# Dilated q and k of the first batch loaded as fp32 by two other queues, and a new order of the work, in a fused sliding-window attention and gated feed-forward kernel

## The chip, the cores and the metric

The kernel runs on one core of a Trainium2 chip. The metric is the device time of one execution in microseconds (us); before the change it is 302.36 us, the median of three runs (302.0 to 302.91). The core has a matrix engine (TensorE, PE in the profile), a vector engine (VectorE, DVE), a scalar engine (ScalarE, ACT), GpSimd (POOL) and a sync engine (SyncE, SP). DMAs are issued by POOL, SP or ACT.

## The reference

Eight batches of eight heads, 576 positions, 64 values per head. Heads 0 to 3 look back over a plain window of 32 positions, heads 4 to 7 over a dilated one: 128 positions back, each fourth of them. The result, 4608 tokens of 512 values, goes through a feed-forward layer with a gate.

```python
def _attn_ref(q, k, v):
    scores = scale * np.matmul(q, k.transpose(0, 1, 3, 2))
    mask_plain = (rel >= 0) & (rel < window)                 # window = 32
    mask_dil = (rel >= 0) & (rel < window * dilation) & (rel % dilation == 0)   # dilation = 4
    ...
    attn = attn / (np.sum(attn, axis=-1, keepdims=True) + 1e-09)
    return np.matmul(attn, v).astype(np.float32)

def _moe_ref(x, w_in, w_out, beta):
    h = x @ w_in                                             # 512 -> 2048
    g = h * (1.0 / (1.0 + np.exp(-beta * h)))
    return (g @ w_out).astype(np.float32)                    # 2048 -> 512
```

## The kernel before

**The feed-forward part** goes over nine tiles of 512 tokens. For each tile, `slot_h` (L904) makes 16 groups: four matmuls (L913; for the first four groups of the first tile six, of parts of the tokens, so 72 instructions in that tile) add up one bank of h from xT (the attention's result, transposed) and w_in; ACT makes a tanh of it (L922), DVE the gate g (L927). A bank of PSUM is held from the first matmul to the end of the gate. `block` (L936) then makes the output of 128 tokens: 16 matmuls (L948, "o") from g and w_out, the first eight with the first half of w_out, the others with the second; an eviction to osb on ACT or DVE (L963, L965) and a store by SP (L968).

**The attention part** runs batch by batch and is laid into the feed-forward matmuls, since a tile of tokens needs its batch's result. For batches 0 to 2 q and k are loaded by row (`direct_qk`, L428, into the tiles st: a dilated part std, a plain part stp), by POOL with a cast from fp32 to bf16 in the DMA. PE transposes them in groups of 36 small matmuls (dilated L500, plain L510); ACT and DVE copy the halves to kT, qT, dk, dq (L262, which is the helper `copy`). Then come scores on PE (dilated L709, plain L773, tail L678), exps on ACT (L645), masks on DVE or POOL (L649; for the first batch PE adds them to the scores, L699, L759, L762), values on PE (dilated L814, plain L830, tail L799), a normalization on DVE (L664, L665), and for batches 0 and 1 transposes back on PE (L852, L867, L882) with copies to xT. From batch 2 on the way back goes by DMA. From batch 3 on, q and k are cast into DRAM by POOL's DMAs and transposed by SP's. The plain values (vp, `direct_vp`, L444) lie in rows of 96 positions with a halo of 32, which DVE or POOL copies on chip once they have landed.

**What sets the order.** Nothing is issued by hand. Each piece is a `plan.op` with its possible engines, guessed durations, dependencies and a due time (`vt`); `Plan.run` (L78) goes through them with a guessed clock of each engine, picks the next piece by time and due time, and so writes the order of each engine's instructions. CAPS (L46) limits how many PSUM banks a kind of work holds at once (of eight in all). NUDGE (L48) shifts the guessed start of single pieces by their number. Where PE would have nothing to do in the first 80 us of that guess, `filler` (L1060) puts in a matmul of zeros (L1061). The order is fixed when the program is built; on the chip each engine goes through its list and waits for what each instruction needs. At most eight DMAs of POOL's queue are open at a time: the ninth waits for the first one's landing.

**The loads of the start.** POOL's DMAs come in this order: dilated q, plain k, plain q, the dilated values (vd), two halves of the plain ones (vp); then batch 1's dilated k, w_in in three pieces (512, 512 and 1024 columns), the two halves of w_out, the tail values (vt), then batch 1's dilated q, plain k and plain q, its values, and so on. Only the dilated k rows of the first batch go another way: `first_keys` (L434) loads them as fp32, half by SP and half by ACT, into a part of the second g buffer (free at that time), and ACT and DVE cast each half to bf16. SP issues beta ahead of its half.

## Time and profile before

| | |
|---|---|
| median of three runs | 302.36 us |
| the profiled execution | 302.0 us, of which the span is 300.3 us |
| mean granted clock of TensorE | 0.994 |
| busy: PE, DVE, ACT, POOL | 291.0, 183.8, 168.8, 86.4 us |
| first h matmul; first o matmul | 20.10; 34.13 us |
| queue 0 (POOL's): bytes moved | 18.58 MB |
| fillers (L1061) | 45 |

The span runs from the first instruction to the last. A line of the table of groups names the source line, the engine, the operation, output and input tiles, the count, then busy time and mean duration, then the idle time of the engine just before these instructions and what ended it. A busy share can hide waits, since matmuls overlap; the start of one set of matmuls and that of the next tell more. In the tables by stage the share of DMA is a sum over transfers that overlap and can exceed 1.

### The profile page before, as it was taken

What the parts mean: (1) busy time and instruction counts of PE and PEld (TensorE: products, weight loads), DVE (VectorE), ACT (ScalarE), POOL (GpSimd) and SP (SyncE); (2) the same over time, 40 slices, a digit from 0 to 9 for tenths busy, and PEclk for the clock granted to TensorE, in tenths of its full rate; (3) what the DMA queues carried; (4) which work ended last, traced back from release to release, by engine and by line L of the source; (5) the groups of instructions that cost most, each with busy time, mean ns of one, the idle gap of its engine ahead of it and who ended that gap; (6) DMA issues with size and microseconds to landing.
All of it is one profiled execution on the core that took longest, in us unless ns stands there. A gap on an engine that the chain in (4) does not pass through costs nothing.

```text
span 300.3 us, 6262 instructions
## 1 busy us (share of the span) xinstructions
PE 291.0 (97%) x2430; PEld 148.2 (49%) x2466; DVE 183.8 (61%) x425; ACT 168.8 (56%) x310; POOL 86.4 (29%) x125
## 2 busy tenths in 40 slices
PE   6999999999999999999999999999999999999995
PEld 3665455645454444544545454445454444444454
DVE  4686667788767756786669365946485047543300
ACT  2677667876567643854386347733674158554311
POOL 8776356384337012710182046200000000000000
PEclk9799999999999999999999999999999999999999
DMA  7999999579999999999999989996203400000122
GB/s 153 183 208 207 202 178 214 144 104 157 200 193 184 149 176 149 199 184 167 180 178 135 224 185 192 145 191 155 76 20 97 110 35 35 2 36 35 56 86 70
DMA packets 111009, 42.00 MB, mean 140 GB/s; under 512 B 87636, under 2 KB 103652, under 8 KB 110980
## 3 DMA queue, kind: packets, MB, share of 16 engines
q0 software_dynamic: 60016, 18.58, 60.0%
q1 hardware_dynamic: 50676, 22.66, 36.3%
q8 instruction: 19, 0.31, 0.4%
q10 hardware_dynamic: 288, 0.36, 0.4%
q14 instruction: 10, 0.08, 0.1%
HBM read 37.76 MB, written 18.87 MB: 189 GB/s over the span
## 4 chain that ended last, share of the span: by engine, by line
PE 94%; DMA 2%; DVE 2%; issue 1%; ACT 0%; DVEq 0%; POOLq 0%
PE bank L948 41%; PE bank L913 41%; DMA st<-in_q_dram 2%; PE bank L830 2%; PE bank L709 2%; PE bank L814 1%; PE bank L1061 1%; PE bank L737 1%; PE bank L500 1%; PE bank L510 1%; PE bank L773 1%; PE bank L799 1%; PE bank L678 1%; DVE xdm L665 1%; DVE pt L649 0%
## 5 line engine op out<-in xcount | busy, mean ns | idle before, releaser
L948 PE MATMUL bank<-w_out_bf,g 128*128 128x512 bf16 (+2 forms) x585 | 132.2, 367 | 1.9 <-issue 1.1
L913 PE MATMUL bank<-xT,w_in_bf 128*128 128x512 bf16 (+2 forms) x571 | 132.2, 376 | 0.6
L927 DVE SCALAR_TENSOR_TENSOR g<-tnh,bank 128x512 bf16<-128x512 bf16 x144 | 95.4, 683 | 53.8 <-ACT tnh L922 52.6
L922 ACT ACTIVATE tnh<-bank,beta_half 128x512 bf16<-128x512 f32 x144 | 96.4, 688 | 50.7 <-PE bank L913 40.6
L913 PEld LDWEIGHTS <-w_in_bf 128*128 128x128 bf16 x584 | 55.7, 98 | 62.5 <-issue 0.3
L948 PEld LDWEIGHTS <-g 128*128 128x128 bf16 x608 | 55.2, 98 | 57.9 <-issue 0.2
L963 ACT ACTIVATE osb<-bank 128x512 f32<-128x512 f32 (+1 forms) x31 | 18.2, 592 | 42.9 <-PE bank L948 40.9
L645 ACT ACTIVATE pt<-bank 128x384 bf16<-128x384 f32 (+1 forms) x54 | 21.0, 464 | 3.8 <-PE bank L737 2.2
L645 ACT ACTIVATE ptd<-bank 128x512 bf16<-128x512 f32 x32 | 17.0, 600 | 8.9 <-PE bank L709 8.8
L649 DVE TENSOR_TENSOR pt<-pt,mask_n 128x384 bf16<-128x384 bf16 (+1 forms) x40 | 13.9, 364 | 12.7 <-ACT pt L645 12.3
L665 DVE TENSOR_TENSOR xsp<-bank,rcp 96x384 bf16<-96x384 f32 x32 | 17.7, 554 | 1.1
L421 POOL DMA_DIRECT2D vt<-in_v_dram x16 | 16.7, 1116 | 0.9 <-PE bank L799 0.9
L664 DVE RECIPROCAL rcp<-bank 128x4 f32<-128x4 f32 (+2 forms) x72 | 12.8, 178 | 5.5 <-PE bank L814 3.4
L649 DVE TENSOR_TENSOR ptd<-ptd,mask_d 128x512 bf16<-128x512 bf16 x28 | 11.2, 421 | 7.7 <-ACT ptd L645 7.1
L665 DVE TENSOR_TENSOR xdm<-bank,rcp 128x256 bf16<-128x256 f32 x32 | 13.6, 424 | 1.1
L965 DVE TENSOR_SCALAR osb<-bank 128x512 f32<-128x512 f32 (+2 forms) x7 | 4.2, 595 | 16.1 <-PE bank L948 16.1
L421 POOL DMA_DIRECT2D vp<-in_v_dram x9 | 11.2, 1249 | 7.2 <-DVE g L927 4.2
L421 POOL DMA_DIRECT2D s<-in_q_dram x10 | 12.6, 1264 | 0.3 <-issue 0.3
L1027 POOL COPY pace<-xT 1x2 bf16<-1x2 bf16 x4 | 0.7, 176 | 41.3 <-DMA xT<-x 41.3
L421 POOL DMA_DIRECT2D s<-in_k_dram x10 | 12.2, 1220 | 0.9 <-issue 0.9
L1061 PE MATMUL bank<-zero 128*128 128x256 bf16 x45 | 9.7, 331 | 1.1 <-DVE warm L321 1.1
L830 PEld LDWEIGHTS <-pt 128*128 128x128 bf16 x192 | 8.6, 97 | 4.4 <-DVE pt L649 0.3
(115 smaller groups left out, 176.2 us busy)
## 6 DMA issues: line engine op xcount, KB each, us to landing
out_dram<-osb SPq DMA_DIRECT2D x35, 256.0 KB, 6.3
s<-in_k_dram POOLq DMA_DIRECT2D x10, 288.0 KB, 10.0
s<-in_q_dram POOLq DMA_DIRECT2D x10, 288.0 KB, 8.5
w_out_bf<-in_moe_w_out_dram POOLq DMA_DIRECT2D x2, 1024.0 KB, 18.5
vp<-in_v_dram POOLq DMA_DIRECT2D x7, 288.0 KB, 13.4
st<-in_q_dram POOLq DMA_DIRECT2D x6, 288.0 KB, 6.8
x<-xsp SPq DMA_DIRECT2D x12, 144.0 KB, 5.2
st<-in_k_dram POOLq DMA_DIRECT2D x5, 288.0 KB, 7.2
```

What stands on the lines that cost most here:

```text
L421: {"POOL": nc.gpsimd, "SP": nc.sync, "ACT": nc.scalar}[queue].dma_start(out=out, in_=in_)
L645: nc.scalar.activation(out=w(), in_=sc(), func=ACT.Exp, scale=SCALE)
L649: E[e].tensor_tensor(out=w(), in0=w(), in1=m(), op=ALU.mult)
L664: nc.vector.reciprocal(out=r, in_=p[..., D])
L665: nc.vector.tensor_tensor(out=dst, in0=p[..., 0:D], in1=r.unsqueeze(len(p.shape) - 1).to_broadcast(list(p.shape[:-1]) + [D]), op=ALU.mult)
L830: nc.tensor.matmul(pv[:, a, h2, :], lhsT=lhs, rhs=vp[kv][:, (2 * x + h2) * NI + 3 * j + a, 0:D + 1], start=True, stop=True)
L913: nc.tensor.matmul(bank(g)[:, a:z], lhsT=w_in_bf[:, kt, fb * P:(fb + 1) * P], rhs=xT[:, kt, xo + a:xo + z], start=(i == 0 and kt == kts[0] ...
L922: nc.scalar.activation(out=th[:, 0:n], in_=bank(g)[:, 0:n], func=ACT.Tanh, scale=beta_half[:, fb:fb + 1])
L927: nc.vector.scalar_tensor_tensor(out=g_t[t % 2][:, fb, c0:c0 + n], in0=th[:, 0:n], scalar=1.0, in1=bank(g)[:, 0:n], op0=ALU.add, op1=ALU.mult)
L948: nc.tensor.matmul(bank(g)[:, lo:hi], lhsT=g_t[t % 2][:, fb, tb * P:(tb + 1) * P], rhs=w_out_bf[:, fb, lo:hi], start=(fb == 0), stop=(fb = ...
L963: nc.scalar.mul(out=ob[:, lo:hi], in_=bank(g)[:, lo:hi], mul=0.5)
L1061: nc.tensor.matmul(BANKS[b][:, 0:256], lhsT=zero[:, 0:P], rhs=zero[:], start=True, stop=True)
```

## The change

1. The dilated q rows of the first batch are loaded like the k rows: as fp32, half by SP and half by ACT, into the next five blocks of the second g buffer, then cast on chip. `first_keys` becomes `first_rows(z)`; q's due time is put just behind k's.
2. The due time of the two w_out loads goes from -7.27 to -7.2, so behind the loads of batch 1's q and k rows (-7.25).
3. h may hold three PSUM banks at once, no longer four.
4. NUDGE is another list of shifts (about a hundred of them, for other pieces).

```diff
-    CAPS = {"h": 4, "p": 4, "o": 3, "z": 4, "a": 8, "s": 5, "w": 6}
+    CAPS = {"h": 3, "p": 4, "o": 3, "z": 4, "a": 8, "s": 5, "w": 6}
-    NUDGE = {7: -400, 18: -2500, 19: -900, 33: -60, 47: -2500, 49: 400, 54: 400, 55: -150, 62: 60,
+    NUDGE = {6: -150, 10: -2500, 17: -900, 19: 400, 22: -150, 27: -2500, 40: -900, 52: 2500, 54: -900,
...
-    def first_keys():
+    def first_rows(z):
-        stage = g_t[1][:, 0:5, :].rearrange("p f n -> p (f n)").bitcast(FP32)[:, 0:RD * D]
-        src = bass.AP(tensor=k.tensor, offset=k[0, 4].offset, ap=[[RD * D, P], [1, RD * D]])
+        stage = g_t[1][:, 5 * z:5 * z + 5, :].rearrange("p f n -> p (f n)").bitcast(FP32)[:, 0:RD * D]
+        src = bass.AP(tensor=(k, q)[z].tensor, offset=(k, q)[z][0, 4].offset, ap=[[RD * D, P], [1, RD * D]])
...
-                        lambda e, x=x: copy(e, std[0][:, part[x]], stage[:, part[x]]),
-                        [load(("SP", "ACT")[x], (stage[:, part[x]], src[:, part[x]]), [], -9.1, 288, .41, 400, 1200)],
-                        -9.1, sbuf=True) for x in range(2)]
+                        lambda e, x=x: copy(e, std[z][:, part[x]], stage[:, part[x]]),
+                        [load(("SP", "ACT")[x], (stage[:, part[x]], src[:, part[x]]), [], -9.1 + .02 * z, 288, .41, 400, 1200)],
+                        -9.1 + .02 * z, sbuf=True) for x in range(2)]
...
-        ld[0]["qk", z, h0] = first_keys() if n == 0 else direct_qk(0, z, h0, [], -9 + .01 * n)
+        ld[0]["qk", z, h0] = first_rows(z) if h0 else direct_qk(0, z, h0, [], -9 + .01 * n)
...
-                 [], -7.27 + .01 * n, 2048, .41)
+                 [], -7.2 + .01 * n, 2048, .41)
```

In the program that is built, this moves on each engine:

- POOL issues plain k, plain q, the values, w_in in three pieces, then batch 1's dilated k, the tail values, batch 1's dilated q, plain k and plain q, then the first half of w_out; the second half follows behind the masks and batch 1's dilated values, and batch 1's plain values follow that. Three memsets for the second batch's values stand early, ahead of the identity matrix.
- SP issues k, q and then beta; ACT issues k and q ahead of its table load. DVE casts three of the four halves, ACT one.
- PE transposes dilated k, plain k, dilated q, plain q, and then makes all 16 dilated scores of the first batch. Batch 1's transposes and scores stand between the h groups 8 to 13 of the first tile, where the old order has them between the first o matmuls; the first o follows after 60 h instructions instead of 68. There are 52 fillers instead of 45: 35 ahead of the first h (37 before) and 17 behind it (8 before), of which eight stand ahead of h group 8, five and two in batch 1's scores.
- From batch 3 on the order of kinds is alike; o matmuls and h groups are more finely mixed.

## The prediction

> **What bounds the kernel now.** I began with the page: busy times, then the slices.

> ```profile
> PE 291.0 (97%) x2430; PEld 148.2 (49%) x2466; DVE 183.8 (61%) x425; ACT 168.8 (56%) x310; POOL 86.4 (29%) x125
> ...
> PE   6999999999999999999999999999999999999995
> ...
> PEclk9799999999999999999999999999999999999999
> DMA  7999999579999999999999989996203400000122
> ```

> TensorE (PE) is busy everywhere but in the first and last slice; the DMA engines are full up to about 50 us and slack later. The costliest groups say what PE does:

> ```profile
> L948 PE MATMUL bank<-w_out_bf,g 128*128 128x512 bf16 (+2 forms) x585 | 132.2, 367 | 1.9 <-issue 1.1
> L913 PE MATMUL bank<-xT,w_in_bf 128*128 128x512 bf16 (+2 forms) x571 | 132.2, 376 | 0.6
> ...
> L1061 PE MATMUL bank<-zero 128*128 128x256 bf16 x45 | 9.7, 331 | 1.1 <-DVE warm L321 1.1
> ```

> h (L913) and o (L948) hardly ever wait. In the chain of waits, four of either take 0.86 us late in the run, 0.216 each, and no line of another engine is there for long after 73 us. So nothing can be won after some 60 us; what can change lies in front. The table by stage:

> ```profile
> 0.00:20.00 20.00, 16.59 (x329) 11.00 (x330) 13.02 (x48) 11.18 (x25) 16.09 (x37) 0.91 1.17 178
> 20.00:40.00 20.00, 19.84 (x151) 10.41 (x153) 12.71 (x24) 12.40 (x21) 10.15 (x15) 1.00 1.24 205
> 40.00:60.00 20.00, 19.41 (x424) 11.82 (x417) 15.62 (x45) 16.02 (x40) 9.92 (x15) 1.00 1.27 176
> ```

> (PE, weight loads, DVE, ACT, POOL, then clock, DMA share, GB/s.) The timeline of PE gives the marks that I count from:

> ```profile
> 7.78 0.48 PE L500 MATMUL bank<-turn,st 64*64 64x64 bf16 x36 [1.92 <-DMA st<-in_q_dram]
> ...
> 20.10 0.38 PE L913 MATMUL bank<-xT,w_in_bf 128*128 128x512 bf16 x1
> ...
> 34.13 1.89 PE L948 MATMUL bank<-w_out_bf,g 128*128 128x512 bf16 x8
> ```

> PE waits 1.92 us for the dilated q rows, starts h at 20.10 and then has work without a break. From 20.10 to the end of the span are 300.3 - 20.1 = 280.2 us.

> The second clock of this stage is POOL's queue. Its timeline, and the DMA views from 20 to 45 and from 30 to 33 us:

> ```profile
> 14.34 1.77 POOL L421 DMA_DIRECT2D w_out_bf<-in_moe_w_out_dram  x2
> ...
> 30.98 1.19 POOL L421 DMA_DIRECT2D vp<-in_v_dram  x1 [2.99 <-DMA w_out_bf<-in_moe_w_out_dram]
> ```
> ```profile
> DMA packets 9494, 4.94 MB, mean 198 GB/s; under 512 B 5842, under 2 KB 8918, under 8 KB 9489
> ...
> q0 software_dynamic: 9489, 4.88, 143.3%
> ```
> ```profile
> vp<-in_v_dram POOLq DMA_DIRECT2D x1, 288.0 KB, 13.4
> ```

> Queue 0 (POOL's) moves nearly all, without a pause, at 198 GB/s counted at the destination. The halves of w_out take 16.4 and 20.6 us, so land at 30.8 and 35.8; the plain values (vp) of the second batch land at 30.98 + 13.4 = 44.4, and PE asks for them at 49.8 only.

> **The change, part by part.** The order of the built program (it holds no times) shows what moves.

> *Dilated q and k of the first batch.* q leaves POOL's queue, where it was first (issue 1.35, landing 7.74), for SP and ACT, as k did already; SP issues k at 0.82 instead of 1.29, beta last. The k halves moved in 1.9 to 4.2 us, up to 392 GB/s of fp32 (3.0 to 3.3 us), about what 198 GB/s of bf16 read from fp32 amount to: q costs the engines the same 1.5 us (288 KB / 198) on either queue. I give the earlier start 0.2 us (bounds 0 and 0.5, the 0.47 between SP's issues). DVE gets two more casts of 0.44; they lie while PE waits for the plain k rows, and would cost 0.9 at the first h if that cover were gone. One more issue of 0.41 stands ahead of ACT's table load; nothing on ACT is due before 3.8.

> [...]

> *The first h.* The new PE order is: transposes of k, plain k, q, plain q, then all sixteen dilated scores. Plain k and q now lead POOL's queue and should land near 7 and 9 (9.1 and 10.6 before), so the scores end near 10, where before the second eight began at 13.2. Then ACT sets the pace: qT 0.64, four exps of 0.60, six of 0.35 and three xT copies (0.40, 0.40, 0.35), 6.3 us, so 16.3. The first w_in columns landed at 10.97 + 7.2 = 18.2; the 288 KB of batch 1's k no longer lie ahead: 16.7. I take 17.0 with handoffs, 3.1 earlier. Bounds: 16.3, and 20.1 (no gain).

> *What PE must do before one mark.* The mark is the first plain values matmul of batch 1 (L830, reading vp). In the new order there lie between first h and mark: 72 h instructions = 16 groups of 0.863, 13.8; 20 o, 4.3; and of attention some 6.0 (four transposes of batch 1 at 0.43, scores of two kinds 1.5, values 0.6 + 0.5, tails 0.6, transposes back 1.1, by rows of 20 to 60 us). Sum 24.1. Fillers (L1061, six in 0.76, so 0.12 each): 52 stand in the new order, 45 in the old; behind the first h 17 against 8. So PE would be at the mark at 17.0 + 24.1 + 2.0 = 43.1.

> *What the queue allows.* Ahead of the second batch's vp now lie the same transfers as before, only in another order (batch 1's rows ahead of w_out) and without q's 288 KB, whose engine time stays. So vp lands at 44.4 - 0.2 = 44.2. The first half of w_out gets 960 KB put before it (batch 1's q and two plain rows at 288, the first batch's tail values at 96): 30.8 + 960/198 - 0.2 = 35.4. The first o therefore cannot start at 34.1 but at 35.4, and from it to the mark PE has 8.5 us (20 o at 0.216, three h groups at 0.863, scores 0.4, values 0.6, transposes back 0.5): 43.9. Two roads give 43.9 and 44.2: **the queue, not PE, sets the mark**, and PE's earlier start of 3.1 us goes into 1.1 us of waiting, 0.86 of work that the old order had ahead of h, and 1.0 more of fillers. POOL's own issues are no bound: the waits for a free slot (eighth transfer before landed) end 10 us or more before a transfer's turn.

> *A new wait at the mark.* Two of the six values matmuls can run; the other four wait for DVE's copy of the halo rows (0.49 for 32x1280), and behind them in PE's order stand the tail's values with the next transfers, 96 KB (0.5). Before, 5 us of slack covered both. I take 0.7; bounds 0 (vp earlier than PE) and 1.7 (POOL's copy takes 1.24 and vt is late).

> *The rest behind the mark.* The 280.2 us hold 8 fillers (1.0); the new order defers six values, the tail score and 36 transposes (0.25 + 0.19 + 0.42 = 0.86) past its first h; 24.1 are ahead of the mark: 280.2 - 1.0 + 0.86 - 24.1 = 256.0.

> *Three banks of h.* A group holds its bank for matmuls 0.86, tanh 0.69, gate 0.68 and handoffs of 0.15: 2.38. Three banks give 3 x 0.863 = 2.59, so 0.2 spare; an eviction of osb (0.60) that comes between makes PE wait 0.4 unless other matmuls stand there. The new order puts o or values between most groups: six runs of four or more groups, fourteen before. Bounds: -1.5 (what L913 loses over ideal from 58 to 282 us, 510 x 2.9 ns) and 36 x 0.4 = 14. I take 0.4, a quarter of the loss seen, its nearest row. The dues of batches 3 to 7 move by a few groups, with 15 us and more between a batch's last values and its first h: nothing.

> **Sum.** 44.2 + 0.7 + 256.0 + 0.4 = 301.3 against 300.3, so +1.0. The profiled execution took 302.0, 1.7 more than its span and 0.36 less than the median; I keep both offsets: 302.36 + 1.0 = 303.4.

> The clock falls to 0.60 and 0.55 in 8 to 12 us (table in steps of 2 us), after PE's wait. [...]

> **Rivals.**
> *Queue alone (25%).* vp lands at 44.2, the halo copy is hidden and three banks cost nothing: 44.2 + 256.0 = 300.2, so 302.3. For it: the mark is near break-even (44.3). Against it: nothing stands between vp and the halo copy.
> *Faster (15%).* The early stretch, where queue 0 moves only 140 to 160 GB/s from 5 to 8 us, gets denser with q off it, and vp lands 1.5 us or more earlier, at 42.7 or less. Then PE decides: 43.1 + 256.0 = 299.1, so 301.2; it decides where vp lands below 43.0. Against it: the same bytes, the same packets of k and q.
> *Banks and mixing (25%).* Batch 1's exps and evictions now run beside h groups (25 to 42 us: on ACT ten tanh 6.9, twelve exps 5.2, four evacuations 2.6, tail and xT copies 2.5, in all 17.2 us of work in 17), and three banks stop h behind them; one in six of the 36 evictions costs 0.4, 2.4 in all in place of my 0.4: 305.4. For it: the new order itself leaves 8 + 5 + 2 fillers there.
> *The change does not do what it says:* the fp32 rows land no earlier and h starts at 20.1; then PE is at the mark at 46.2, 302.2 in span, 304.3; I count it in the last case.

> **Numbers.** Forecast 303.4 (35%; own range 302.8 to 304.2, a third of it within 0.3%). The measurement tells about 0.3%, 0.9 us, from no change: 301.45 to 303.27. Faster 15%, same 25 + 10 = 35%, slower 25 + 25 = 50%. The range from 301.3 to 305.8 leaves out the far part of the two outer cases.

> **What would show it.** First h at 16.3 to 18; fillers 52; first o near 35.4, waiting for w_out; values of batch 1 near 44.2 after a wait for vp or DVE's halo copy; after 60 us h and o at 0.216. Wrong if PE waits for ACT or DVE by more than 1 us between 25 and 42, if vp lands below 43, or if L913's idle time grows by several us.

## The result, and the profile after

The changed kernel takes 302.96 us in the median of 20 runs, and the kernel before, run in turn with it on the same chip, 302.04. The ratio is 1.0035, with a 95% interval of 1.0023 to 1.0047: slower by 0.9 us, a little more than the 0.3% that can be told from no change. The forecast was 1.0 us slower.

The page of the changed kernel (span 300.9, before 300.3). Its line numbers are four less than before: h is L909, o L944, the filler L1057, the plain values L826.

```profile
PE 292.0 (97%) x2433; PEld 148.8 (49%) x2473; DVE 188.0 (63%) x432; ACT 168.6 (56%) x304; POOL 86.1 (29%) x125
...
PE   7899999999999999999999999999999999999995
...
PEclk9799999999999999999999999999999999999999
DMA  7999999899989994999999999997043100101112
...
L944 PE MATMUL bank<-w_out_bf,g 128*128 128x512 bf16 (+2 forms) x589 | 137.1, 368 | 1.1 <-issue 0.3
L909 PE MATMUL bank<-xT,w_in_bf 128*128 128x512 bf16 (+1 forms) x563 | 136.0, 376 | 1.4 <-issue 0.2
```

h and o together wait as little as before (1.4 + 1.1 us in all, before 0.6 + 1.9), and the clock row is the same. The difference lies in front; the timeline of PE gives the marks:

```profile
8.43 0.48 PE L506 MATMUL bank<-ident_b,st 64*64 64x64 bf16 x36 [1.65 <-DMA st<-in_k_dram]
...
11.38 1.03 PE L705 MATMUL bank<-dq,dk 64*128 64x128 bf16 x16
...
18.10 1.03 PE L909 MATMUL bank<-xT,w_in_bf 128*128 128x512 bf16 x3
...
25.23 1.04 PE L1057 MATMUL bank<-zero 128*128 128x256 bf16 x8
...
32.52 0.71 PE L1057 MATMUL bank<-zero 128*128 128x256 bf16 x5
...
36.40 1.03 PE L944 MATMUL bank<-w_out_bf,g 128*128 128x512 bf16 x4
...
44.92 0.34 PE L826 MATMUL bank<-vp,pt 128*128 128x65 bf16 x6
...
282.56 14.92 PE L944 MATMUL bank<-w_out_bf,g 128*128 128x512 bf16 x98
```

h starts 2.0 us earlier (18.10, before 20.10), the mark (the first plain values matmul of batch 1) is reached at 44.92, and the last stretch of o starts at 282.56. In the kernel before that stretch is this line:

```profile
282.34 14.92 PE L948 MATMUL bank<-w_out_bf,g 128*128 128x512 bf16 x99
```

So of the 0.6 us between the two spans PE's work makes 0.22; the other 0.38 are the last store, 3.0 us from issue to the end of the span where it was 2.6. Both values occur in the kernels below, under either order of the work, so I put nothing on it. A profile is one execution: the spans of the changed kernel's 20 runs go from 300.7 to 302.6. Small differences are therefore judged by the ratios, and profiles are used for where time goes.

POOL's queue (issues from its timeline; KB and us to landing from the DMA views):

```profile
18.83 0.88 POOL L417 DMA_DIRECT2D w_out_bf<-in_moe_w_out_dram  x1 [1.56 <-DMA w_in_bf<-in_moe_w_in_dram]
...
26.70 1.19 POOL L417 DMA_DIRECT2D vp<-in_v_dram  x1
```
```profile
w_out_bf<-in_moe_w_out_dram POOLq DMA_DIRECT2D x1, 1024.0 KB, 16.7
...
vp<-in_v_dram POOLq DMA_DIRECT2D x1, 288.0 KB, 17.1
```

The 1.56 us of the first line are a wait for the landing of a w_in piece, the transfer that stands eight ahead of it in this queue. By these lines w_out's first half lands at 18.83 + 16.7 = 35.5, batch 1's plain values at 26.70 + 17.1 = 43.8. PE takes the one 0.9 and the other 1.1 us later, without a wait at either place.

### The profile page after: what moved, and what is told of

Same layout as the page of the kernel before. It is cut to its first block, busy times and chain, and to the rows that moved or that the text cites. A ratio compares the mean times of both kernels' runs of the same rounds, so it can differ in the third digit from the quotient of the medians.

```text
span 300.9 us, 6293 instructions
## 1 busy us (share of the span) xinstructions
PE 292.0 (97%) x2433; PEld 148.8 (49%) x2473; DVE 188.0 (63%) x432; ACT 168.6 (56%) x304; POOL 86.1 (29%) x125
## 4 chain that ended last, share of the span: by engine, by line
PE 94%; DMA 2%; issue 1%; DVE 1%; DVEq 0%; POOLq 0%
PE bank L944 41%; PE bank L909 41%; DMA st<-in_k_dram 2%; PE bank L826 2%; PE bank L705 2%; PE bank L1057 1%; PE bank L810 1%; PE bank L733 1%; PE bank L506 1%; PE bank L769 1%; PE bank L496 1%; PE bank L795 1%; PE bank L878 0%; PE bank L674 0%; PE bank L863 0%
## 5 line engine op out<-in xcount | busy, mean ns | idle before, releaser
L944 PE MATMUL bank<-w_out_bf,g 128*128 128x512 bf16 (+2 forms) x589 | 137.1, 368 | 1.1 <-issue 0.3
L909 PE MATMUL bank<-xT,w_in_bf 128*128 128x512 bf16 (+1 forms) x563 | 136.0, 376 | 1.4 <-issue 0.2
L918 ACT ACTIVATE tnh<-bank,beta_half 128x512 bf16<-128x512 f32 x144 | 97.5, 688 | 64.4 <-PE bank L909 56.3
L923 DVE SCALAR_TENSOR_TENSOR g<-tnh,bank 128x512 bf16<-128x512 bf16 x144 | 97.0, 684 | 57.7 <-ACT tnh L918 57.0
L909 PEld LDWEIGHTS <-w_in_bf 128*128 128x128 bf16 x584 | 55.4, 98 | 61.9
L944 PEld LDWEIGHTS <-g 128*128 128x128 bf16 x608 | 54.9, 98 | 56.3
L959 ACT ACTIVATE osb<-bank 128x512 f32<-128x512 f32 (+1 forms) x31 | 18.3, 591 | 28.8 <-PE bank L944 28.6
L645 DVE TENSOR_TENSOR pt<-pt,mask_n 128x384 bf16<-128x384 bf16 (+1 forms) x38 | 13.8, 376 | 11.8 <-ACT pt L641 11.5
L641 ACT ACTIVATE ptd<-bank 128x512 bf16<-128x512 f32 x32 | 17.2, 603 | 6.2 <-PE bank L705 6.2
L661 DVE TENSOR_TENSOR xdm<-bank,rcp 128x256 bf16<-128x256 f32 x32 | 13.6, 424 | 1.1
L417 POOL DMA_DIRECT2D vp<-in_v_dram x9 | 12.1, 1347 | 0.8 <-DMA vp<-in_v_dram 0.8
L417 POOL DMA_DIRECT2D vt<-in_v_dram x16 | 12.3, 772 | 0.0
L1057 PE MATMUL bank<-zero 128*128 128x256 bf16 x52 | 10.5, 334 | 1.2 <-DVE warm L317 1.1
L826 PEld LDWEIGHTS <-pt 128*128 128x128 bf16 x192 | 8.9, 97 | 4.9
## 6 DMA issues: line engine op xcount, KB each, us to landing
out_dram<-osb SPq DMA_DIRECT2D x35, 256.0 KB, 2.6
s<-in_q_dram POOLq DMA_DIRECT2D x10, 288.0 KB, 8.7
s<-in_k_dram POOLq DMA_DIRECT2D x10, 288.0 KB, 7.9
w_out_bf<-in_moe_w_out_dram POOLq DMA_DIRECT2D x2, 1024.0 KB, 16.4
vp<-in_v_dram POOLq DMA_DIRECT2D x7, 288.0 KB, 13.6
st<-in_k_dram POOLq DMA_DIRECT2D x5, 288.0 KB, 12.6
st<-in_q_dram POOLq DMA_DIRECT2D x5, 288.0 KB, 12.8
```

The lines of the kernel that those rows point to most:

```text
L417: {"POOL": nc.gpsimd, "SP": nc.sync, "ACT": nc.scalar}[queue].dma_start(out=out, in_=in_)
L641: nc.scalar.activation(out=w(), in_=sc(), func=ACT.Exp, scale=SCALE)
L645: E[e].tensor_tensor(out=w(), in0=w(), in1=m(), op=ALU.mult)
L661: nc.vector.tensor_tensor(out=dst, in0=p[..., 0:D], in1=r.unsqueeze(len(p.shape) - 1).to_broadcast(list(p.shape[:-1]) + [D]), op=ALU.mult)
L826: nc.tensor.matmul(pv[:, a, h2, :], lhsT=lhs, rhs=vp[kv][:, (2 * x + h2) * NI + 3 * j + a, 0:D + 1], start=True, stop=True)
L909: nc.tensor.matmul(bank(g)[:, a:z], lhsT=w_in_bf[:, kt, fb * P:(fb + 1) * P], rhs=xT[:, kt, xo + a:xo + z], start=(i == 0 and kt == kts[0] ...
```

## The experiments

In all of them the order that the planner wrote is kept as a list `seq` of pieces and engines, and only the list is edited; so one part moves and the rest stays. "Lag" is how much later one of the 144 gates (DVE, the line that writes g) starts than the same gate in the parent's profile. Apart from single gates it stays constant within 0.01 us between two events, and so shows where time is lost. An "evictor" is the instruction of ACT or DVE that empties a bank.

### The fillers behind the first h

```diff
+    h1 = next(n for n, (o, e) in enumerate(seq) if o and e == "PE" and getattr(o.group, "kind", "") in ("h", "p"))
+    seq = [x for n, x in enumerate(seq) if x[0] or n < h1]
```

On the changed kernel:

> The changed kernel with its order of work kept, but without the 17 filler matmuls behind its first h (the fillers multiply zeros and write no result that is read). Theory P (PE's own list of work sets the mark): the fillers are 17 x 0.12 = 2.0 us of that list, so the first o comes as soon as w_out's first half is there (35.5), and the mark, the first plain values matmul of batch 1, moves forward from 44.9 until it meets batch 1's plain rows (landed 43.8): span 300.9 - 0.5 to - 1.1 = 299.8 to 300.4. Theory Q (the POOL queue already sets the mark, as recorded): the mark stays at 44.4 or later and PE waits at the first o or at the mark; span 300.4 to 300.9. Rival W: the fillers stand where PE would wait for evictions anyhow: the mark stays at 44.9 and the span at 300.9. Rival C: without them the granted clock falls between 20 and 45 us (1.00 now): span over 301.

On the kernel before:

> The kernel before with its order kept, but without the 8 filler matmuls behind its first h. There the batch-1 rows land 5 us ahead of their use (44.4 against 49.8) and w_out's first half 3.3 us ahead of the first o, so no queue stands in the way. Theory P: the whole 8 x 0.12 = 1.0 us is won: span 299.3, ratio to the kernel before 0.997. Rival W (the fillers stand in waits for evictions of the spread x or of transposes): nothing, 300.3. Rival C: the clock falls between 20 and 32 us and the span grows over 300.5.

The changed kernel without its 17 fillers took 304.74 us, ratio to the kernel before 1.0078 (1.0050 to 1.0106): slower still, by 2.5 us in span. The kernel before without its eight took a ratio of 1.0004 (0.9987 to 1.0021), as W had it. P falls, and Q's price too; for the changed kernel W and C hold together. PE's timeline of the first:

```profile
26.23 1.02 PE L909 MATMUL bank<-xT,w_in_bf 128*128 128x512 bf16 x4 [0.51 <-DVE g L923]
...
31.89 0.21 PE L506 MATMUL bank<-ident_b,st 64*64 64x64 bf16 x1
33.13 0.47 PE L506 MATMUL bank<-ident_b,st 64*64 64x64 bf16 x35 [1.03 <-issue]
...
34.38 0.43 PE L769 MATMUL bank<-qT,kT 64*128 64x96 bf16 x6 [0.55 <-ACT qT L258]
```

The first line is the h group behind the eight fillers, at 26.11 with them: most of their 1.04 us stood in a wait for a gate. The second and third are one group of transposes, cut after the first of 36 by 1.03 us that no engine's work explains (see below). After these idle times the clock falls, to a half from 35.0 to 38.4 us (table by stage; the last columns are clock, DMA share, GB/s):

```profile
34.00:36.00 2.00, 1.40 (x15) 0.77 (x16) 1.97 (x6) 2.00 (x5) 0.00 (x0) 0.75 1.36 202
36.00:38.00 2.00, 1.78 (x10) 0.60 (x10) 1.33 (x4) 0.81 (x3) 1.28 (x2) 0.50 1.25 210
```

The lag is 0.33 from the first gate on and 0.12 behind the place of the eight fillers, so these cost 0.21; it goes to 1.35 at the cut, to 2.52 by 42 us, and stays there. Five of the six executions show a mean clock of 0.994 and spans of 302.9 to 304.2, the sixth 1.000 and 301.6: in this one execution without the fall most of the loss is gone.

### Is it the queue?

```diff
+    half = Op([], lambda e: dma("POOL", w_out_bf[:, 0:4, :], moe_w_out[0:4 * P, :].rearrange("(c p) d -> p c d", p=P)), ...)
+    seq = [(half, e) if o is w_out_ld[0] else (o, e) for o, e in seq]
```

> The changed kernel with its order kept, but w_out's first half is loaded to one half only (512 KB instead of 1024; the other half of those weights is set to zero, so part of the output matmul's result is left out). PE's list is the same. Everything behind it on POOL's queue, and the half itself, lands 2.6 us earlier (512 / 198): w_out 32.9, batch 1's plain rows 41.2. Theory Q (the queue sets the mark, as recorded): the mark leaves 44.9 and goes to PE's own time, 1 us or more earlier; span 299.2 to 299.9. Theory R (formed from the run without fillers: PE's list with the waits in which its fillers stand decides, and the queue has 0.5 to 0.9 us to spare everywhere): nothing, 300.7 to 301.1.

The other half of these weights is zero here, so this kernel leaves part of the output out.

```profile
w_out_bf<-in_moe_w_out_dram POOLq DMA_DIRECT2D x1, 512.0 KB, 13.8
...
vp<-in_v_dram POOLq DMA_DIRECT2D x1, 288.0 KB, 14.4
```
```profile
36.70 1.03 PE L944 MATMUL bank<-w_out_bf,g 128*128 128x512 bf16 x4
...
45.22 0.34 PE L826 MATMUL bank<-vp,pt 128*128 128x65 bf16 x6
```

The transfers were issued at 18.89 and 26.61 and landed at 32.7 and 41.0, 2.8 us earlier than in the changed kernel. The first o and the mark did not follow: 36.70 and 45.22, each 0.3 later, the lag that this run has from its first gate on. The ratio is 1.0029 (1.0014 to 1.0044), the changed kernel's own within its interval. **Q falls:** the queue doesn't set the mark.

### Is it the third bank?

```diff
+    gone, at = pe[i:i + 8], pe[i + 8]            # the eight fillers at 25.2 us, and the h group behind them
+    g, spare = seq[at][0].acquire[0], seq[gone[-1]][1]
+    ...
+    seq = [... for n, (o, e) in enumerate(seq) if n not in gone]    # from here on the two banks change names
```

> The changed kernel with its order kept, but at one place, 25.2 us, the h group behind the eight fillers takes the bank of these fillers as a fourth h bank, instead of the one that the gate of the group before last frees, and the eight fillers are gone. Theory B (three banks cost about 0.9 us here): PE is 0.9 earlier at batch 1's first transposes; of this 0.3 to 0.6 remain where the plain k rows of batch 1 (landed 29.7, used at 30.02) and then plain values (43.8, used at 44.92) come next; mark 44.4, span 300.3 to 300.6. Theory Q: the queue takes all but 0.3 of it: 300.6 to 300.9. Rival C (any idle PE or fewer fillers cost clock, as in the run without fillers): the span grows over 301.2.

The ratio is 1.0057 (1.0038 to 1.0076). The h group now follows at once, and the next piece waits in its place:

```profile
14.85 0.39 PE L1057 MATMUL bank<-zero 128*128 128x256 bf16 x2 [1.07 <-ACT pt L641]
...
27.15 0.48 PE L496 MATMUL bank<-turn,st 64*64 64x64 bf16 x36 [0.55 <-DVE g L923]
...
32.91 0.48 PE L506 MATMUL bank<-ident_b,st 64*64 64x64 bf16 x36 [0.98 <-ACT ptd L641]
...
115.59 2.76 PE L909 MATMUL bank<-xT,w_in_bf 128*128 128x512 bf16 x12 [0.80 <-DMA xT<-x]
```

Batch 1's first transposes start at 27.15, with three banks at 27.06. This run was 0.34 behind from its first gate on (the stand of the first line), and is 0.09 behind here: so 0.25 was won and not 0.9; with three banks and without these eight fillers it was 0.21 already (above). Theory B falls for this place: PE waits at 25 to 27 us for the row of gates (in the changed kernel five in 3.11 us, from 22.7 on), now one piece later. The edit passes one bank on and makes no ninth, and the changed kernel with a limit of four everywhere was not built. C's number came (span 303.0), but not by the clock, which was 1.00 until the end; the loss is 0.98 at 32.91, and 0.8 at a wait for a transposing DMA of xT, until 115.59.

### The dilated q rows alone

Taken out of the changed kernel:

```diff
+    q_op = Op([], lambda e: dma("POOL", std[1], bass.AP(tensor=q.tensor, ...)), ...)
+    seq = [(q_op, "POOL")] + [x for x in seq if x[0] not in gone]     # gone: q's two loads and two casts
```

> The changed kernel with its order kept, but with batch 0's dilated q back as one casting transfer at the head of POOL's queue, without the two DVE casts. This undoes the first part of the change alone. Theory P: plain k and plain q land 0.7 to 1.5 us later again (9.1 and 10.6 us as before, against 8.35 and 9.86), q itself at about 7.7 is needed second and delays nothing, so the first h comes 0.5 to 1.0 later (18.6 to 19.1) and, as nothing behind it has slack but the fillers' own gaps, the span grows by 0.5 to 1.0: 301.4 to 301.9. Theory Q (the queue sets the mark): all of POOL's queue is 0.69 later by the one more issue, or not at all, since the same bytes are read either way: span 300.9 to 301.6, and an h that starts later costs nothing by itself.

Put into the kernel before, in two ways:

```diff
+        if o in k_ld:                                  # first try: q ahead of k on each queue
+            new += [x for x in loads_q if x[1] == e]
```

> The kernel before with its order kept, but with batch 0's dilated q in fp32 in two halves on SP's and ACT's queues ahead of k's halves, cast by DVE. The first part of the change alone, put into the kernel before. PE's first wait (1.92 us, until 7.78, for the q rows) then ends with q's casts at about 5, and the plain rows of POOL's queue land 0.7 to 1.5 us earlier (8.4 and 9.9). Theory P: the first h comes 0.7 to 1.5 earlier than 20.10 unless ACT or DVE hold it; the work behind it follows, span 298.8 to 299.6. Theory Q: in this kernel no queue binds behind the first h, so the same. Rival N (the start is bound by ACT's own list and by the w_in columns, landed 18.2 before): the first h moves by no more than 0.3 and the span stays at 300.0 to 300.3.

```diff
+        new.append((o, e))                             # second try: k, q, and beta last on SP
+        if o in k_ld:
+            new += [x for x in loads_q if x[1] == e]
+            new += [(beta_ld, "SP")] if e == "SP" else []
```

> The kernel before with its order of matmuls kept, with dilated q of batch 0 in fp32 on SP's and ACT's queues behind k's halves and beta last on SP, as the changed kernel has it (the earlier try had q ahead of k and beta first, and k's SP half landed at 8.1 only). q's casts end at about 6.9 and k's at 5.7, so PE's first transposes start at 6.9 instead of 7.78, the plain rows land 0.7 earlier (8.4 and 9.9). Theory P or R: first h 0.3 to 0.7 earlier, span 299.6 to 300.0, ratio to before 0.998. Rival N (ACT's and DVE's evictions and the w_in columns, landed 18.2, hold the first h): 300.2 to 300.4. Rival C (the clock falls at another place and takes the gain): over 300.6.

Without the fp32 rows the changed kernel's first h came at 19.15, 1.05 later, and the lag was 1.05 to the last h, as theory P had it: 1.0057 (1.0036 to 1.0079). So this part is worth 1.05 us in these profiles, more than the 0.2 that I gave it: plain k and q land 0.75 earlier (8.35 and 9.86, in the kernel before 9.1 and 10.6). The ratios differ by 0.7 us (1.0057 - 1.0035), but their intervals overlap. In the kernel before, the first try lost, which no theory had, since SP's half of k, now behind beta and q, was there at 8.1 only: 1.0032 (1.0011 to 1.0054). The second brought the first h 0.86 earlier, but the end only 0.17, and the ratio is 1.0002 (0.9985 to 1.0018). It lost 0.81 here, amid the dilated values of one bank, and 0.4 more in the same way at 45.9:

```profile
13.36 0.23 PE L814 MATMUL bank<-vd,ptd 128*128 128x65 bf16 x2
14.39 0.48 PE L814 MATMUL bank<-vd,ptd 128*128 128x65 bf16 x10 [0.81 <-issue]
...
45.94 0.59 PE L948 MATMUL bank<-w_out_bf,g 128*128 128x512 bf16 x2 [0.24 <-issue]
```

### The order of the queue alone

Taken out of the changed kernel, and put into the kernel before:

```diff
+    wo = [w_out_ld[0], w_out_ld[2]]
+    seq = [x for x in seq if x[0] not in wo]
+    seq = seq[:n + 1] + [(o, "POOL") for o in wo] + seq[n + 1:]   # first case: behind w_in
...
+        seq.insert(n + 1, (o, "POOL"))                            # second: behind batch 1's plain q, and its dilated values
```

> The changed kernel with its order of matmuls kept, but with both halves of w_out directly behind w_in on POOL's queue, ahead of batch 1's rows, as before. This undoes the second part of the change alone. Batch 1's dilated k rows then land some 10 us later (2 x 5.05 us of transfer; 24.9 becomes about 35), and PE, whose order has their transposes at 27.06, ahead of most of the other work, waits there for about 8 us. All theories: span 307 to 310 and a lower granted clock behind the wait. If it is under 302, the order of the queue is no part of what this change does.

> The kernel before with its order of matmuls kept, with w_out's halves put behind batch 1's rows on POOL's queue (the first behind the plain q rows, the second behind the dilated values), as the changed kernel has them. The second part of the change alone. The same bytes move; w_out's first half lands at about 35.4 and its second at about 42, where the first o of this order stands at 34.13 and needs the second half before 42. Theory (order of matmuls and order of the queue belong together): PE waits 1.3 us at the first o and up to 2 more at the second half; span 301.5 to 303.5. Rival (the order of the queue alone makes the difference between the two kernels): span 300.5 to 301.0, the same as the changed kernel.

```profile
35.56 0.70 PE L496 MATMUL bank<-turn,st 64*64 64x64 bf16 x36 [8.65 <-DMA st<-in_k_dram]
```
```profile
36.05 2.92 PE L948 MATMUL bank<-w_out_bf,g 128*128 128x512 bf16 x8 [2.29 <-DMA w_out_bf<-in_moe_w_out_dram]
```

The first took 313.28 us, 1.0362 (1.0334 to 1.0389), with the wait of 8.65 us for batch 1's rows; the second 305.85, 1.0131 (1.0105 to 1.0156), with 2.29 us at the first o and a half clock from 36.8 to 40.2 behind it. Both spans (311.4 and 304.3) lie over the ranges I had given. Either order of the queue is right for its own order of matmuls and wrong for the other; neither is faster put into the other kernel.

### Stands that no engine explains

In six runs PE stood still where nothing that it needed was late, mostly in the middle of a group. The profile calls this "issue", or names an evictor that had ended long before. Counted in the built programs, the stands come before instruction 449, 961 or 1217 of PE's list, that is 449 + 256 n. PE has 4975 instructions (4974 records in the two fullest traces), and each trace has 19 loads of 16 KB on a queue that the page names instruction (`q8 instruction: 19, 0.31, 0.4%`). I read this as blocks of 256; no record says which instructions a load holds. From the trace's DMA records:

| run | instruction | load, us | PE goes on, us | after the load's end |
|---|---|---|---|---|
| no late fillers | 961 | 30.75 to 31.64 | 33.13 | 1.49 |
| half of w_out | 449 | 12.14 to 13.08 | 14.60 | 1.52 |
| fourth bank | 449; 961 | 12.43 to 13.38; 30.48 to 31.37 | 14.85; 32.91 | 1.47; 1.53 |
| before, q behind k | 449; 1217 | 12.01 to 12.96; 43.24 to 44.49 | 14.39; 45.94 | 1.43; 1.45 |
| changed kernel | 449 | 12.08 to 13.03 | 14.48, no stand | 1.45 |

(Without late fillers, PE also stood before 449, for 0.82 us, and went on 1.24 after its load.) Theory I, formed from this: a block can run some 1.4 us after its load (1.43 to 1.53 in the table), and PE's list of many small instructions is ahead of the loads. Two kernels test it by moving instruction 449 to another place:

```diff
+        if o is None and new and new[-1][0] is None:   # two fillers of 256 columns
+            new[-1] = ("wide", e)                      # become one of 512
+    lone = [n for n, (o, e) in enumerate(new) if o is None][:4]
+    seq = [x for n, x in enumerate(new) if n not in lone]
```

> The changed kernel with its order kept, but each two fillers of 256 columns that stand together are one of 512 columns, and the first four single ones are gone. This takes 22 instructions out of PE's list ahead of the first h. Theory I (PE's instructions come in blocks of 256; in five traces PE stood still before instruction 449 or 961 or 1217 of its list, each time until some 1.4 us after an instruction load of 16 KB had ended): in the runs without fillers and with half of w_out PE stood at instruction 449, a filler ahead of the last dilated values, until 14.6 to 14.85. Now 449 lies behind these values and the transposes back; these run at 13.6 to 14.0 instead of 14.8 to 15.3, any stand is before the second of the two addends that follow, and the first h comes 0.3 to 0.8 earlier (17.3 to 17.8), span 300.1 to 300.6. Rival E (evictions on ACT and DVE set the first h): first h at 18.1 to 18.4, span 300.8 to 301.2. Rival C (fewer fillers let the clock fall at a place without cover): over 301.2.

> The kernel before with its order kept, with dilated q of batch 0 in fp32 behind k on SP and ACT (as tried before, where the first h came 0.9 earlier in spite of a stand of 0.81 at instruction 449 among the dilated values), and with the fillers paired to 512 columns and the first four single ones gone. Theory I: instruction 449 now lies behind the dilated values, which run through by 13.9; the transposes back follow at 14.5 instead of 15.4, the first h at 18.3 to 18.8 against 20.1 before; 0.4 of it may be lost again at instruction 1217 (about 45 us). Span 298.8 to 299.6, ratio to before 0.995 to 0.998: faster than both kernels. Rival E (evictions or the w_in columns, landed 18.2, hold the first h at 19.0 to 19.3): 300.0 to 300.4, ratio 1.000. Rival C (the clock): over 300.5.

The changed kernel with paired fillers:

```profile
14.14 0.39 PE L863 MATMUL bank<-ident_b,xdm 128*128 128x128 bf16 x4
...
17.39 1.03 PE L909 MATMUL bank<-xT,w_in_bf 128*128 128x512 bf16 x4
...
31.04 0.26 PE L506 MATMUL bank<-ident_b,st 64*64 64x64 bf16 x8
32.12 0.41 PE L506 MATMUL bank<-ident_b,st 64*64 64x64 bf16 x28 [0.82 <-issue]
```

The stand at 449 is gone, the transposes back run at 14.14 and the first h comes at 17.39, as I's range said. But instruction 961 now lies within batch 1's transposes: 0.82 are lost there, the lag goes from -0.72 to +0.28, and the ratio is 1.0046 (1.0030 to 1.0062). In the kernel before, with q in fp32 and paired fillers, PE stood (0.42 us) exactly before 449, at its new place behind the dilated values, and went on 1.25 after that load's end:

```profile
14.71 0.22 PE L759 MATMUL bank<-add_F,ident_b 128*128 128x96 bf16 x1 [0.42 <-ACT pt L645]
...
18.77 0.38 PE L913 MATMUL bank<-xT,w_in_bf 128*128 128x512 bf16 x1
```

The first h came at 18.77 and the last h 0.67 earlier. The medians do not show it: 1.0009 (0.9990 to 1.0027). I's places and times held in both; its gain at the end held in neither ratio. One more count speaks for I: in the four fullest traces (half of w_out, w_out first, fourth bank, and q behind k) none of 72 blocks began less than 1.25 us after the end of its load, wherever PE stood at that time.

### A version put together

```diff
+    seq = [x for n, x in enumerate(seq) if x[0] not in (None, "wide") or n < h1]    # on top of the last one
```

> The kernel before with its order kept, dilated q in fp32 behind k on SP and ACT, paired fillers, and no filler behind the first h: the version put together from the tries on the kernel before (profiles: 0.67 earlier at the last h from the first two together, 0.13 from the last alone). If these add up: first h 18.6 to 18.9, last h 0.7 to 0.9 earlier than in the kernel before, span 299.3 to 300.0, ratio 0.997 to 0.999. Rival G (what PE wins in front is given back between 37 and 60 us, at the block of instructions that begins with number 1217 and at evictions, as in both tries): ratio 1.000 to 1.002. Rival C (fewer fillers, the clock falls behind a wait): over 1.003.

The median is 301.61 us beside 301.88 of the kernel before: 0.9985 (0.9963 to 1.0008), and the span 299.6, as forecast. Its last stretch of o starts a full microsecond earlier than in the kernel before:

```profile
281.34 14.92 PE L948 MATMUL bank<-w_out_bf,g 128*128 128x512 bf16 x100
```

The way there was not the forecast one: the first h came at 19.44, not at 18.6 to 18.9, in an execution with half clock from 7.9 to 11.3 and without a stand, and what was won in front was not lost again behind. Its interval lies below that of the changed kernel; against the kernel before it isn't settled.

## Why the prediction was right, and where it was not

The forecast held, and in part by luck. That PE's earlier start is spent again before the end was right; that it is spent in waiting for POOL's queue was wrong. Of the sum 44.2 + 0.7 + 256.0 + 0.4 = 301.3, the profile has 44.92 for the first term, nothing for the second, 255.98 for the third, and nothing that could be told apart for the fourth: 300.9. The first term was too small and the second and fourth too large, and these errors cancelled. For the first step below one more line, from ACT's timeline in the changed kernel:

```profile
11.45 0.64 ACT L258 COPY qT<-bank 128x576 bf16<-128x576 bf16 x1 [0.27 <-PE bank L506]
```

1. *First h at 17.0:* it came at 18.10, 1.1 later. ACT set the pace, as I had it; from its copy of qT to the first h it took 6.65 us, idle for 0.67 of them, where I had 6.3 and 0.7. But it began late. Plain k and plain q led POOL's queue, yet its first packet moved at 5.20 us only (before 3.65), while the fp32 halves of k and q moved until 5.8; they landed at 8.35 and 9.86, not near 7 and 9. Then the half clock (8.9 to 12.3 us) stretched the transposes (0.69 and 0.70 us for 36 of them, 0.48 at full clock just before), and the scores ran from 11.38 to 12.41 instead of ending near 10. In three runs without it PE stood at instruction 449 (see above) until 14.6 to 14.85 and the first h came at 18.2 to 18.4 just the same. With neither, in the run with paired fillers, it came at 17.39.
2. *"The queue, not PE, sets the mark":* wrong. The landings were as worked out (w_out 35.5 for 35.4, plain values 43.8 for 44.2), but with both 2.8 us earlier the mark stayed. PE came there by its own list: 18.10 + 26.82, where I had 17.0 + 26.1. The 26.1 (24.1 of work and 17 fillers) was near; of the 0.7 that are left PE's idle time from the first h to the mark makes 0.58, in small pieces (0.22 of it from 31 to 36.4 us). My 1.1 us of waiting for the queue are the 1.1 by which h started late: that the two are equal is chance.
3. *1.0 for nine more fillers:* the size held, the nature didn't. They take little time of their own (0.21 for the eight at 25 us); they fill waits for gates and evictions that batch 1's attention meets among the h groups. Taken out, the waits stayed, and in the changed kernel the clock fell (to 0.50, from 35.0 to 38.4 us).
4. *Deferred work, 0.86; rest behind the mark, 256.0:* measured 300.9 - 44.92 = 255.98 (0.38 of it the late last store).
5. *Halo wait, 0.7:* none; all six values matmuls ran at once.
6. *Three banks, 0.4:* at most 0.8 over the whole run (L909 idles 1.4 us, with no single cause over 0.2, where L913 had 0.6), and a fourth bank at one place moved the wait to the next piece.
7. *The fp32 rows, 0.2:* 1.05 by the profiles, 0.7 by the medians (not clear of noise).
8. *The clock:* it fell for the same 3.41 us as before, half a microsecond later (8.9 to 12.3 us, before 8.4 to 11.8). The sum has no term for it, and it does not show in the first h: in three traces without the fall the stand at 449 took its place (first h at 18.2 to 18.4, with the fall at 18.10).

So where did the two microseconds go? PE's last stretch starts 0.22 later though h starts 2.0 earlier, which makes 2.2. By my estimate 0.86 are work put off. Nine more fillers make 1.1, at 25 to 36 us, where batch 1's transposes and scores now stand among the h groups; about 0.3 is left. Whether that stretch can be passed faster is not shown: three tries that freed it from fillers or brought PE there earlier (fourth bank, no late fillers, paired fillers) lost 0.8 to 1.0 us in it, but each at the same instruction 961, whose load began at 29.8 to 30.8 us in them and at 27.6 in the changed kernel. Nor was the new order of matmuls built without the other parts.

Of the rivals, "banks and mixing" named that place rightly and overpriced it (2.4 us and 305.4). "Faster" was to decide where the plain values land below 43.0; with half of w_out they landed at 41.0, and nothing came of it. "Queue alone" (302.3) falls with the queue. The plain rows did land earlier, so the change did what it says. Of the signs of being wrong, none came: the plain values landed at 43.8, L909 idled 0.8 us more, and PE shows no wait of 1 us from 25 to 42, though 16 fillers cover waits there.

What stays open: PE's last work is only 0.22 later in the profiles, and the medians differ by 0.9. The clock of the untraced executions gives a hint. Both profiles have a mean clock of 0.994. Of the changed kernel's 20 executions eight have 0.994 and spans of 301.15 in the mean; the twelve with 0.998 or more have 301.5, so full clock gains nothing there. In the kernel before it does: in the four sets that ran in turn with the experiments, the executions with 0.993 or 0.994 took 0.5 to 1.4 us more in the mean than those with 0.998 or more (18 and 66 executions in all). A stand at instruction 449 at full clock, as in three traces of the changed order, would explain that, but no trace of either kernel was taken at full clock, so it is not shown.

## What to carry to other kernels

An earlier start is worth only what the tightest stretch behind it lets through: follow the lag of one kind of instruction through both traces, and the stretch shows itself as a step. Fillers that a planner put in are not free time, since they mark waits; of three versions without the late ones, the clock fell behind a wait in one. Take one out only together with the wait that it covers. An order of loads and an order of matmuls are one decision, and testing one without the other tells that they fit, not which is faster. And a number that comes out right does not show that its terms were right.

## What the runs showed of the hardware

The half clock came in stretches of 3.41 us at a place that differs from run to run: the kernel before (wait in front 1.92) has one from 8.4 to 11.8, the changed kernel (wait in front 1.65) from 8.9 to 12.3, and three runs of the changed order with waits of 1.7 to 2.0 us have none there. The changed kernel without late fillers has one from 35.0 to 38.4, and the kernel before with w_out late one from 36.8 to 40.2. What sets the place is not shown.
